# A spectral filter feeding a SwiGLU block: signs carried by the products instead of an in-place sign change, row scales sent at once, and an input fetch moved behind the second bounce

## The chip, the cores and the metric

The kernel runs on one core of a Trainium2 chip. The metric is the device time of one execution in microseconds (us), lower is better.

Engine names as the profile gives them: PE is TensorE (matmul), PEld its weight loads, DVE is VectorE, ACT is ScalarE, POOL is GpSimd, SP is SyncE, which here only issues DMAs.

## The reference

```python
X = np.fft.rfft(x, axis=1)                       # x: (8, 3008, 256) float32
Y = X * (filt_r + 1j * filt_i)[None]             # filters: (1505, 256)
x = np.fft.irfft(Y, n=3008, axis=1).reshape(8 * 3008, 256)
rms = np.sqrt(np.mean(x * x, axis=-1, keepdims=True) + 1e-06)
xn = x / rms * rms_g
g = xn @ w_gate                                  # (256, 1536)
out = (g / (1 + np.exp(-g)) * (xn @ w_val)) @ w_out
```

## The kernel before

The eight batches (called inputs too) go through one software pipeline. The feed-forward part of batch `b` fills TensorE, and the FFT of batch `b+1`, done as matmuls in two steps, is threaded between its pieces. One **slot** is one tile of 128 hidden features of a block of 512 tokens: four gate and value matmuls (`pg`, `pv`), and two slots later the `down` matmuls (`po`). A batch has 6 blocks of 12 slots, 72 slots. A plan says in which slot each piece of the FFT, the filter and the normalization is issued:

```python
items = [(b, m, jt) for b in range(B) for m in range(6) for jt in range(JT)]
...
for i in range(len(items) + 4):
    if i < len(items):
        gv(*items[i])                       # gate, value, silu, product
    for fn, a in plan.get(i, ()):           # the threaded pieces of slot i
        fn(*a)
    if 2 <= i < len(items) + 2:
        down(*items[i - 2])
    ...
    for fn, a in late.get(i, ()):           # q_unit only
        fn(*a)
```

The slots are only an order of issue: each engine works its own queue in that order and runs ahead until it must wait. In the profile of the kernel before, POOL had the block that slot 72 reads ready at 184.9 us, and PE came to it at 187.2. The pieces that matter here:

```python
def x_load(b, c):        # input fetch, issued by POOL: two DMAs a chunk, four chunks
def a_unit(b, i, ...):   # first transform: one matmul (psa), copied out by ACT or DVE to t1
def z_store(b, c):       # first bounce: t1 to DRAM, issued by SP; t1 has two buffers here
def t2_load(b, c):       # second bounce: back in the other layout, issued by SP

def b_unit(b, i):        # second transform and filter
    ps = bank(3, "psb")                     # one PSUM bank for all filter units
    ... two matmuls ...
    nc.vector.tensor_tensor(out=s1, in0=ps, in1=f1, op=ALU.mult)         # batches 2 to 7
    ...                  # batch 1: both products on DVE; for four units on POOL,
                         # from a copy v that ACT makes of the bank

def negate(c, r, n):     # called four times during batch 1
    t = fi[c][HALF:P, r:r + n, :]
    nc.gpsimd.tensor_scalar(out=t, in0=t, scalar1=-1.0, scalar2=None, op0=ALU.mult)

def swap_unit(b, i, h):  # batches 2 to 7: the crossed product, one half at a time
    a, e = ...           # 64 partitions out, the other 64 in
    nc.vector.tensor_tensor(out=s2[a], in0=ps[e], in1=f2[e], op=ALU.mult)
    if h:
        nc.gpsimd.tensor_tensor(out=s, in0=s1, in1=s2, op=ALU.add)

def bi_unit(b, i):       # inverse matmuls (psi), copied by ACT to t3 (two buffers)
def g_store(b, c):       # t3 to DRAM, issued by SP
def n_unit(b, m, dh):    # last inverse step of a block of 512 tokens

def q_unit(b, m):        # row sums of squares by PE, then
    nc.gpsimd.tensor_tensor(out=rho, in0=u, in1=mhalf, op=ALU.pow)
def rho_move(b, m):      # the row scale to DRAM, issued by POOL
def rho_load(b, m):      # back, spread over all partitions (rb), issued by SP
def xn_unit(b, m):       # POOL: xn = y * rb, the block that pg and pv read

def scale_split(m): ...  # the same spread without DRAM, by DVE and PE;
def scale_apply(m, bk):  # used for the first two blocks of batch 0 only
```

Batch 2's plan sets its filter units at `b_at = [71 + 3 * i ...]` and its first transform at `a_at = [51, 52, 53, 53, 54, 54, 55, 55, 56, 56, 57, 58]`; batch 3's fetch starts at slot 61.

## Time and profile before

| | before |
|---|---|
| median of the runs | 935.75 us (931.08 to 936.64, 4 runs) |
| span of the profiled run | 932.2 us |
| PE, DVE, ACT, POOL busy | 95%, 72%, 66%, 45% |

The page of the profile gives the span, and the busy time of each engine with its share of the span and its count of instructions:

```profile
span 932.2 us, 17516 instructions
...
PE 886.1 (95%) x6321; PEld 560.8 (60%) x6321; DVE 674.0 (72%) x1070; ACT 619.8 (66%) x1048; POOL 415.8 (45%) x359
```

PE is the bound: it is busy 299.3 of the 300 us from 500 to 800 us. What can be won lies before 215 us. The list of waits of PE alone, from 62 to 215 us, names it: who waited for what, us in total, how many times, the longest. In this kernel L263 is POOL's product of a filter unit, L241 a filter unit's matmul, L204 the first transform, L286 the inverse.

```profile
PE psi L286 <- POOL s L263: 6.9, 1, 6.9
PE psb L241 <- DMA t<-z_tmp: 5.5, 1, 5.5
PE psa L204 <- DVE t L207: 3.0, 1, 3.0
PE psi L286 <- POOL s L277: 2.0, 1, 2.0
```

These are the four stalls that the prediction calls S1, S3, S2 and S4, in this order. The timeline of POOL before S1 shows what kept it (start, duration, instruction; in brackets how long it stood idle before and what released it). L345 is the power that makes the row scale, L350 its sending, L405 the normalization, L269 the sign change:

```profile
90.21 1.03 POOL L345 TENSOR_TENSOR rho<-u,mhalf 128x4 f32<-128x4 f32 x1 [5.54 <-DVE u L343]
91.35 2.89 POOL L405 TENSOR_TENSOR xn<-y,rb 128x1024 f16<-128x1024 f32 x1
94.19 0.62 POOL L350 DMA_DIRECT2D r_tmp<-rho  x1
...
103.55 2.87 POOL L405 TENSOR_TENSOR xn<-y,rb 128x1024 f16<-128x1024 f32 x1 [4.67 <-DMA rb<-r_tmp]
...
108.15 5.39 POOL L269 TENSOR_SCALAR fi<-fi 64x2048 f32<-64x2048 f32 x1
113.62 1.26 POOL L263 TENSOR_TENSOR s<-v,fr 128x512 f16<-128x512 f32 x1
```

The scale of the power at 90.21 us is ready at 91.24 but is sent at 94.19 only, because the normalization of another block stands between. It is used at 103.55. Then comes the sign change, and only at 113.62 the product that PE needs. The table by windows shows the clock (the column after the bracketed counts is PEclk, then the DMA engines' busy share and GB/s; the first numbers are the window and the busy us of PE, PEld, DVE, ACT, POOL):

```profile
115.00:120.00 5.00, 4.16 (x16) 2.11 (x16) 1.29 (x2) 1.19 (x2) 4.78 (x6) 0.50 0.78 150
...
160.00:165.00 5.00, 2.27 (x8) 1.16 (x8) 1.98 (x3) 0.00 (x0) 0.00 (x0) 0.70 0.86 334
180.00:185.00 5.00, 0.68 (x5) 0.29 (x3) 1.05 (x2) 0.49 (x1) 2.99 (x2) 1.00 1.05 242
185.00:190.00 5.00, 3.83 (x15) 1.94 (x15) 1.45 (x3) 1.06 (x2) 1.74 (x4) 0.66 0.61 76
```

After S1, S2 and S3 the granted clock falls to 0.50 to 0.70, so in this profile each stall is paid for after it has ended, too. In the windows in which PE stands in S2 and S3 (160 and 180 us) the DMA engines are 0.86 and 1.05 busy.

### The profile page before, as it was taken

What the parts mean: (1) busy time and instruction counts of PE and PEld (TensorE: products, weight loads), DVE (VectorE), ACT (ScalarE), POOL (GpSimd) and SP (SyncE); (2) the same over time, 40 slices, a digit from 0 to 9 for tenths busy, and PEclk for the clock granted to TensorE, in tenths of its full rate; (3) what the DMA queues carried; (4) which work ended last, traced back from release to release, by engine and by line L of the source; (5) the groups of instructions that cost most, each with busy time, mean ns of one, the idle gap of its engine ahead of it and who ended that gap; (6) DMA issues with size and microseconds to landing.
All of it is one profiled execution on the core that took longest, in us unless ns stands there. A gap on an engine that the chain in (4) does not pass through costs nothing.

```text
span 932.2 us, 17516 instructions
## 1 busy us (share of the span) xinstructions
PE 886.1 (95%) x6321; PEld 560.8 (60%) x6321; DVE 674.0 (72%) x1070; ACT 619.8 (66%) x1048; POOL 415.8 (45%) x359
## 2 busy tenths in 40 slices
PE   8699698789999999999999999999999999999997
PEld 5565454556556666666666666666666666666554
DVE  7866465478888787787878887787878887555554
ACT  7667355557757776687657776687657775576543
POOL 7843774335633664256523555155522554033300
PEclk9999899999999999999999999999999999999999
DMA  9496736535555334553464345542353222321201
GB/s 200 83 169 165 127 65 166 136 71 147 118 143 158 79 96 144 156 110 106 91 179 109 97 97 116 155 101 84 72 173 83 63 63 71 100 63 46 69 24 45
DMA packets 79922, 101.17 MB, mean 109 GB/s; under 512 B 8144, under 2 KB 56464, under 8 KB 79452
## 3 DMA queue, kind: packets, MB, share of 16 engines
q1 hardware_dynamic: 69420, 83.71, 32.7%
q0 software_dynamic: 10416, 16.35, 11.4%
q8 instruction: 49, 0.80, 0.4%
q14 instruction: 37, 0.30, 0.1%
HBM read 67.93 MB, written 46.79 MB: 123 GB/s over the span
## 4 chain that ended last, share of the span: by engine, by line
PE 79%; DVE 6%; DMA 6%; POOL 4%; issue 3%; ACT 2%; SPq 0%; POOLq 0%; ACTq 0%; DVEq 0%
PE po L438 24%; PE pg L421 23%; PE pv L421 22%; DVE hh L426 3%; PE psb L241 2%; PE psi L286 2%; PE psn L318 2%; DMA fr<-in_filt_r_dram 2%; PE psa L204 2%; DMA rb<-r_tmp 2%; DVE o L444 1%; DVE s L274 1%; DMA t<-z_tmp 1%; PE psq L339 1%; POOL xn L405 1%
## 5 line engine op out<-in xcount | busy, mean ns | idle before, releaser
L426 DVE TENSOR_TENSOR hh<-pv,sg 128x512 f16<-128x512 f32 (+1 forms) x576 | 391.7, 680 | 216.3 <-ACT sg L425 103.3
L425 ACT ACTIVATE sg<-pg 128x512 f16<-128x512 f32 (+1 forms) x576 | 338.9, 588 | 248.8 <-PE pg L421 237.2
L438 PE MATMUL po<-wo,hh 128*128 128x256 f16 x2256 | 345.7, 273 | 2.7 <-DVE o L444 0.6
L421 PE MATMUL pg<-xn,wg 128*128 128x512 f16 (+1 forms) x1152 | 339.1, 376 | 0.6 <-POOL xn L405 0.4
L421 PE MATMUL pv<-xn,wv 128*128 128x512 f16 (+1 forms) x1152 | 338.7, 376 | 0.0
L438 PEld LDWEIGHTS <-hh 128*128 128x128 f16 x2256 | 217.4, 98 | 106.0 <-issue 10.4
L277 POOL TENSOR_TENSOR s<-s,s 128x512 f16<-128x512 f16 x96 | 110.5, 1151 | 291.8 <-DVE s L274 238.3
L421 PEld LDWEIGHTS <-wv 128*128 128x128 f16 x1152 | 112.8, 98 | 132.5 <-issue 2.5
L405 POOL TENSOR_TENSOR xn<-y,rb 128x1024 f16<-128x1024 f32 (+1 forms) x46 | 128.8, 2799 | 65.9 <-DMA rb<-r_tmp 59.0
L274 DVE TENSOR_TENSOR s<-psb,fi 64x512 f16<-64x512 f32 x192 | 132.1, 688 | 5.9
L421 PEld LDWEIGHTS <-wg 128*128 128x128 f16 x1152 | 109.4, 98 | 13.7 <-issue 1.3
L291 ACT ACTIVATE t<-psi 96x512 f16<-96x512 f32 x112 | 66.5, 593 | 21.1 <-PE psi L286 15.6
L345 POOL TENSOR_TENSOR rho<-u,mhalf 128x4 f32<-128x4 f32 (+1 forms) x48 | 48.7, 1014 | 69.6 <-DVE u L343 69.5
L324 ACT ACTIVATE y<-psn,gsb 128x512 f32<-128x512 f32 (+1 forms) x94 | 63.8, 679 | 9.0 <-PE psn L318 2.1
L247 DVE TENSOR_TENSOR s<-psb,fr 128x512 f16<-128x512 f32 x96 | 65.4, 681 | 5.9 <-PE psb L241 5.9
L330 ACT ACTIVATE sq<-psn 128x512 f16<-128x512 f32 (+1 forms) x94 | 54.7, 582 | 0.0
L286 PE MATMUL psi<-s,wi 128*128 128x256 f16 x248 | 45.9, 274 | 7.9 <-POOL s L263 6.9
L241 PE MATMUL psb<-t,wb 96*128 96x256 f16 x224 | 43.4, 275 | 9.3 <-DMA t<-z_tmp 5.5
L209 ACT ACTIVATE t<-psa 128x512 f16<-128x512 f32 x71 | 42.4, 597 | 9.5 <-PE psa L204 4.7
L286 PEld LDWEIGHTS <-wi 128*128 128x128 f16 x248 | 24.3, 98 | 36.0 <-issue 11.0
L318 PEld LDWEIGHTS <-t 128*128 128x128 f16 x368 | 28.4, 98 | 20.4 <-issue 0.4
L189 POOL DMA_DIRECT2D xc<-in_x_dram x64 | 34.4, 551 | 4.8 <-DMA wo<-in_moe_w_out_dram 1.3
(97 smaller groups left out, 494.0 us busy)
## 6 DMA issues: line engine op xcount, KB each, us to landing
out_dram<-o SPq DMA_DIRECT2D x84, 256.0 KB
xc<-in_x_dram POOLq DMA_DIRECT2D x56, 192.0 KB, 6.7
rb<-r_tmp SPq DMA_DIRECT2D x42, 256.0 KB
z_tmp<-t SPq DMA_DIRECT2D x28, 384.0 KB
t<-z_tmp SPq DMA_DIRECT2D x28, 384.0 KB
g_tmp<-t SPq DMA_DIRECT2D x56, 192.0 KB
t<-g_tmp SPq DMA_DIRECT2D x21, 384.0 KB
out_dram<-o SPq DMA_DIRECT2D x12, 192.0 KB
```

What stands on the lines that cost most here:

```text
L241: nc.tensor.matmul(ps[:, u, :], w[:, k, :], t, start=True, stop=True)
L247: nc.vector.tensor_tensor(out=s1, in0=ps, in1=f1, op=ALU.mult)
L274: nc.vector.tensor_tensor(out=s2[a], in0=ps[e], in1=f2[e], op=ALU.mult)
L277: nc.gpsimd.tensor_tensor(out=s, in0=s1, in1=s2, op=ALU.add)
L286: nc.tensor.matmul(ps[:, u, :], wi_at(q, 2 * i + u), ss[q][:, u, :], start=(q == 0), stop=(q == n - 1))
L291: nc.scalar.activation(out=st[b]["t3"][c][:, 2 * r:2 * r + 2, :], in_=ps[0:KR], func=AXT.Copy)
L324: nc.scalar.activation(out=y[:, dh, 0:w], in_=ps[:, 0:w], func=AXT.Identity, scale=gsb[:, dh:dh + 1])
L405: nc.gpsimd.tensor_tensor(out=xv, in0=yv, in1=rv.unsqueeze(1).to_broadcast([P, 2, n, P]), op=ALU.mult)
L421: nc.tensor.matmul(ps[:, 0:w], wt[:, dt_, ts(jt, P)], xn[:, dt_, 0:w], start=(dt_ == 0), stop=(dt_ == 1))
L425: nc.scalar.activation(out=sg[:, 0:w], in_=pg[:, 0:w], func=AXT.Silu)
L426: nc.vector.tensor_tensor(out=hh[:, 0:w], in0=pv[:, 0:w], in1=sg[:, 0:w], op=ALU.mult)
L438: nc.tensor.matmul(po[s4 // 2][:, s4 % 2, :], hh[:, ts(s4, P)], wo[:, jt, :], start=(jt == 0 and s4 % 2 == 0), stop=(jt == JT - 1 and (s4 ...
```

## The change

Three parts. The sign moves into the product: one of the two crossed products becomes a `scalar_tensor_tensor` with -1, and the four sign changes on POOL go. The row scale is sent by POOL right behind its power, and in batches 0 and 1 loads and uses come one slot later. Batch 3's fetch moves from slot 61 to 73, behind the second bounce of batch 2; with it batch 2's first transform is stretched, its second bounce comes two slots and its first filter unit one slot later, and one block of batch 1 is normalized earlier.

```diff
-    def negate(c, r, n):
-        t = fi[c][HALF:P, r:r + n, :]
-        nc.gpsimd.tensor_scalar(out=t, in0=t, scalar1=-1.0, scalar2=None, op0=ALU.mult)
 ...
     def swap_unit(b, i, h):
-        nc.vector.tensor_tensor(out=s2[a], in0=ps[e], in1=f2[e], op=ALU.mult)
+        if h:
+            nc.vector.tensor_tensor(out=s2[a], in0=ps[e], in1=f2[e], op=ALU.mult)
+        else:
+            nc.vector.scalar_tensor_tensor(out=s2[a], in0=ps[e], scalar=-1.0, in1=f2[e],
+                                           op0=ALU.mult, op1=ALU.mult)
 ...                                     # end of q_unit; rho_move goes
-        st[b]["u"][m] = rho
+        if b or m > 1:
+            nc.gpsimd.dma_start(r_d[b, m, 0:n * P]..., rho[:, 0:n])
+        else:
+            st[b]["u"][m] = rho
 ...                                     # slots of power, sending, load, use
-            norm_plan(0, m, s0, s0 + 2, r)                     # r = (2, 3, 4, 7)
+            norm_plan(0, m, s0, s0 + 2, (2, 5, 8))
-                          (2, 4, 6, 10) if b > 1 else (2, 3, 4, 7))
+                          (2, 6, 10) if b > 1 else (2, 5, 8))
 ...                                     # batch 1
-                n_at, n_step = [58, 62, 74, 86, 95, 107], 3
+                n_at, n_step = [58, 62, 66, 86, 95, 107], 3    # and step 2 for m < 3
 ...                                     # batch 2
-                a_at = [51, 52, 53, 53, 54, 54, 55, 55, 56, 56, 57, 58]
-                on_dve = (0, 1, 3, 5, 7, 9, 10, 11)
-                b_at = [71 + 3 * i for i in range(16)]
+                a_at = [51, 52, 53, 53, 54, 54, 57, 57, 58, 59, 60, 61]
+                on_dve = (0, 1, 3, 5, 7, 8, 9, 10, 11)
+                b_at = [72] + [71 + 3 * i for i in range(1, 16)]
 ...                                     # batch 3: first transform, fetch
-                a_at = [72, 73, 80, 81, 83, 84, 92, 93, 101, 102, 104, 105]
+                a_at = [77, 78, 80, 81, 83, 84, 92, 93, 101, 102, 104, 105]
-                at(b_at[0] - (5 if b == 1 else 7) + ... t2_load, b, c)
+                at(b_at[0] - (5, 6, 7)[min(b, 3) - 1] + ... t2_load, b, c)
-                at(s0 + lag, bi_unit, b, i)
-                if b == 1 and i in (3, 7, 11, 15):
-                    at(s0 + 2, negate, i // 4, 0, 8)
+                at(s0 + lag - (b == 2 and i == 0), bi_unit, b, i)
-                    at((24, 61)[b - 1] + 2 * c if b < 3 else ..., x_load, b + 1, c)
+                    at((24, 73)[b - 1] + 2 * c if b < 3 else ..., x_load, b + 1, c)
```

More of the change, by code (lines that the diff above doesn't have):

```diff
@@ L345, in q_unit @@
         nc.gpsimd.tensor_tensor(out=rho[:, 0:n], in0=u[:, 0:n], in1=mhalf[:, 0:n], op=ALU.pow)
-        st[b]["u"][m] = rho
-    def rho_move(b, m):
-        n = nq(b, m)
-        nc.gpsimd.dma_start(r_d[b, m, 0:n * P].rearrange("(p q) -> p q", q=n),
-                          st[b]["u"].pop(m)[:, 0:n])
+        if b or m > 1:
+            nc.gpsimd.dma_start(r_d[b, m, 0:n * P].rearrange("(p q) -> p q", q=n), rho[:, 0:n])
+        else:
+            st[b]["u"][m] = rho
     def rho_load(b, m):
@@ L698, in norm_plan @@
                 at((s0, s1)[dh] + 1, sq_unit, b, m, dh)
-            for d, fn in zip(r, (q_unit, rho_move, rho_load, xn_unit)):
+            for d, fn in zip(r, (q_unit, rho_load, xn_unit)):
                 at(s1 + d, fn, b, m)
@@ L708 @@
         at(20, open_sp)
-        for m, s0, r in ((2, 4, (2, 3, 4, 7)), (3, 15, (2, 3, 4, 7)), (4, 19, (2, 3, 4, 7)),
-                         (5, 23, (2, 3, 4, 7))):
-            norm_plan(0, m, s0, s0 + 2, r)
+        for m, s0 in ((2, 4), (3, 15), (4, 19), (5, 23)):
+            norm_plan(0, m, s0, s0 + 2, (2, 5, 8))
         for b in range(1, B):
@@ L737 @@
             for c in range(4):
-                at(b_at[0] - (5 if b == 1 else 7) + (1 if b == 1 else 2) * c if c < 3 else b_at[4] + 1,
+                at(b_at[0] - (5, 6, 7)[min(b, 3) - 1] + (1 + (b > 1)) * c if c < 3 else b_at[4] + 1,
                    t2_load, b, c)
@@ L752 @@
                 for c in range(NXC):
-                    at((24, 61)[b - 1] + 2 * c if b < 3 else a_at[3 * c + 2] + 2, x_load, b + 1, c)
+                    at((24, 73)[b - 1] + 2 * c if b < 3 else a_at[3 * c + 2] + 2, x_load, b + 1, c)
             for c in range(4):
@@ L756 @@
             for m in range(6):
-                step = 2 if b == 1 and m < 2 else n_step
+                step = 2 if b == 1 and m < 3 else n_step
                 norm_plan(b, m, n_at[m], n_at[m] + step,
-                          (2, 4, 6, 10) if b > 1 else (2, 3, 4, 7))
+                          (2, 6, 10) if b > 1 else (2, 5, 8))
         stores = {}
```

## The prediction

> **What bounds the kernel now.** TensorE. The profile page gives PE 886.1 us busy in a span of 932.2 (95%), DVE 72%, ACT 66%, POOL 45%. The table by windows gives PE at least 99.7% busy in each 100 us from 400 to 800 us: nothing to win there. Of the idle PE, about 14 us lie in the first 62 us, untouched, and about 22 us between 62 and 200 us. Its waits and timeline name four stalls there:
>
> - S1, 107.7 to 116.2 us: PE waits 6.92 and 0.84 us for POOL's products of the second input. POOL was late: it waited for a row scale (xn at 103.55; its scale was sent at 94.19 only, behind the xn at 91.35, though the power ended at 91.2), then did one in-place sign change of 5.39 us.
> - S2, 157 to 162.7 us: 0.93 + 3.04 us for evictions that wait for the first bounce (z store) of batch 2, 6.85 us in flight while the 16 DMA engines are full (share 1.0, 267 to 334 GB/s), partly with batch 3's input.
> - S3, 180.7 to 186.2 us: 5.49 us for the second bounce's load, 10.26 us in flight, behind four input fetches issued at 174.2 (DMA share 1.05).
> - S4, 196 to 197.4 us: 2.04 us for POOL's add behind an xn that waited 6.63 us for its row scale.
>
> After S1 to S3 the granted clock is about half for 3 to 6 us (windows: 0.50, 0.70, 0.66). [...] I estimate that S1 costs 10.9, S2 5.2, S3 7.5 and S4 2.1 us: 25.7 in all.
>
> **What changes.** Removed: four sign changes (5.4 us each, 21.5 us of POOL); only the first is on the critical path. Added: nothing on PE; 96 tensor_tensor of 64x512 (688 ns) on DVE become scalar_tensor_tensor. [...] I expect 0.69 us still. Moved: each row scale's DMA follows its power directly (about 3 us sooner for batch 0's fifth); batch 2's last two chunks of the first transform 3 to 4 slots later; the second bounce's loads 2 slots, its use 1 slot later; batch 3's fetch 12 slots later, behind those loads, its use 5 slots later.
>
> **Gains.** S1: POOL's product should be ready near 106.5, before PE asks at 107.7: about 10.5 won. S2: about 4.5. S3: about 6.5. S4: about 2. New costs: batch 3's first fetch is now only 4 slots (about 7.5 us) ahead of its use, behind an xn on POOL, with 6.3 us from issue to landing in this region: a PE wait of 2 to 3 us there, and small waits for POOL's first adds. Net about 20.5 us.
>
> **Predicted: 915 us, 8 in 10 between 908 and 925.** Faster by over 2%: 0.57; within 2%: 0.42; slower: 0.01.
>
> **Shown right by**: no 6.9 us PE wait on POOL; no PE wait over 2 us on the second bounce; clock above 0.95 from 105 to 200 us; DVE swaps all at 0.69 us; PE busy 99.7% later. **Wrong if**: the fetch of batch 3 stalls PE over 4 us (throttling it again); [...] the z stores are slow anyway.

## More of the kernel before

A verdict of "faster" needs 2%.

## The result, and the profile after

| | before | after |
|---|---|---|
| median of the runs | 935.75 us (931.08 to 936.64, 4 runs) | 919.98 us (919.79 to 921.92, 4 runs) |
| ratio | | 0.9851, 95% interval 0.9819 to 0.9883 |
| span of the profiled run | 932.2 us | 918.0 us |

Ratios here and below are taken from the runs of the same rounds. They are not quite the ratio of the quoted medians, which is 0.983 here. The interval lies clear of 1: about 1.5% less.

The page after. Line numbers after the sign change's place are 2 lower than before (L421 is L419, L405 is L403), and the swapped products are L273 and L271 where they were L274.

```profile
span 918.0 us, 17505 instructions
...
PE 885.4 (96%) x6321; PEld 561.2 (61%) x6321; DVE 674.5 (73%) x1071; ACT 619.7 (68%) x1047; POOL 394.8 (43%) x355
```

PE's busy time has not changed (886.1 and 885.4 us). The 14 us came out of its idle time. The list of PE's waits from 62 to 215 us:

```profile
PE psb L241 <- DVE s L271: 3.1, 4, 2.4
PE pg L419 <- POOL xn L403: 2.4, 1, 2.4
...
PE psa L204 <- DMA xc<-in_x_dram: 0.8, 1, 0.8
```

None of the four lines shown of before is left. In their place stand a wait for POOL's normalization, and waits of a filter unit for DVE. POOL's timeline at the place of S1:

```profile
93.27 1.03 POOL L345 TENSOR_TENSOR rho<-u,mhalf 128x4 f32<-128x4 f32 x1 [5.53 <-DVE u L343]
94.60 0.60 POOL L347 DMA_DIRECT2D r_tmp<-rho  x1 [0.29 <-POOL rho L345]
...
96.25 2.92 POOL L403 TENSOR_TENSOR xn<-y,rb 128x1024 f16<-128x1024 f32 x1
...
103.89 2.92 POOL L403 TENSOR_TENSOR xn<-y,rb 128x1024 f16<-128x1024 f32 x1
106.71 1.32 POOL L263 TENSOR_TENSOR s<-v,fr 128x512 f16<-128x512 f32 x1
```

The scale is sent at 94.60, 0.3 us after its power has ended, ahead of the normalization. The next normalization (103.89) finds its scale landed, no sign change follows, and the product is started at 106.71. The windows answer to those of before, the first at S1, the other at the new waits:

```profile
110.00:115.00 5.00, 5.00 (x36) 3.32 (x35) 3.55 (x6) 2.90 (x6) 2.71 (x3) 1.00 1.02 216
...
170.00:175.00 5.00, 3.46 (x13) 1.70 (x13) 1.29 (x2) 0.66 (x2) 3.10 (x3) 0.66 0.23 64
```

The clock is full at S1, but 0.66 from 170 to 175 us. The timeline of PE shows what stands there (from 175 to 180 us, where the clock is 1.00, a pair of gate matmuls of this size takes 0.59 us):

```profile
171.54 1.01 PE L419 MATMUL pg<-xn,wg 128*128 128x512 f16 x2 [2.44 <-POOL xn L403]
...
178.94 0.39 PE L241 MATMUL psb<-t,wb 96*128 96x256 f16 x2 [2.41 <-DVE s L271]
...
184.95 0.38 PE L204 MATMUL psa<-xc,tb 128*128 128x512 f16 x1 [0.78 <-DMA xc<-in_x_dram]
```

Three new waits stand there: 2.44 us for the first normalized block of batch 1 (L419, slot 72), 2.41 us of batch 2's second filter unit for DVE (L241, slot 74), and 0.78 us for batch 3's fetch (L204). The first of them, and why it was late, on POOL:

```profile
159.56 1.03 POOL L345 TENSOR_TENSOR rho<-u,mhalf 128x4 f32<-128x4 f32 x1 [23.59 <-DVE u L343]
160.89 0.64 POOL L347 DMA_DIRECT2D r_tmp<-rho  x1 [0.30 <-POOL rho L345]
...
168.64 2.85 POOL L403 TENSOR_TENSOR xn<-y,rb 128x1024 f16<-128x1024 f32 x1 [2.58 <-DMA rb<-r_tmp]
```

The power at 159.56 is followed at once by its sending (160.89), and the scale lands in DRAM at 162.7. SP issues its load at 162.77 and two loads of the second bounce at 163.3 and 163.7. From 165 to 170 us the DMA engines are 1.01 busy, and the normalization (168.64), which waits for the scale's load, ends at 171.5.

To see where the time went, one can take from each trace the start of the first gate matmul of some slots. The table gives the length of a stretch in the two profiled runs of each kernel (the second pair are the runs `before_again` and `after_again` of below), and the difference of the means:

| stretch | before, two runs | after, two runs | difference |
|---|---|---|---|
| start to slot 34 | 107.0, 110.4 | 110.0, 109.6 | +1.1 |
| 34 to 40 (S1) | 21.4, 19.7 | 10.8, 10.8 | -9.8 |
| 40 to 60 (S2) | 39.4, 38.2 | 33.4, 33.4 | -5.4 |
| 60 to 71 | 12.1, 12.1 | 13.8, 13.8 | +1.7 |
| 71 to 72 (S3) | 7.3, 7.2 | 3.6, 3.3 | -3.8 |
| 72 to 75 | 5.9, 6.3 | 8.1, 8.4 | +2.1 |
| 75 to 77 (S4) | 5.0, 4.8 | 2.8, 2.8 | -2.1 |
| 77 to 84 (fetch of batch 3) | 11.9, 11.9 | 13.4, 14.1 | +1.8 |
| 84 to 575 | 714.1, 714.2 | 714.1, 714.2 | 0.0 |

The sum is -14.4 us. S1, S2 and S4 gave what the prediction said, within 1 us. From slot 60 to 84, where it expected 6 us (6.5 for S3, 2 for S4, less 2.5 for the fetch), 0.3 us were won. Some of that is only moved work: the plan puts pieces of the transform and of the normalization into slots 60 to 71 that stood elsewhere. In `after_a_early` below, which moves the pieces of the transform back, the stretch from 60 to 71 is 12.8 us, 1.0 less.

### The profile page after: what moved, and what is told of

Same layout as the page of the kernel before. It is cut to its first block, busy times and chain, and to the rows that moved or that the text cites. A ratio compares the mean times of both kernels' runs of the same rounds, so it can differ in the third digit from the quotient of the medians.

```text
span 918.0 us, 17505 instructions
## 1 busy us (share of the span) xinstructions
PE 885.4 (96%) x6321; PEld 561.2 (61%) x6321; DVE 674.5 (73%) x1071; ACT 619.7 (68%) x1047; POOL 394.8 (43%) x355
## 4 chain that ended last, share of the span: by engine, by line
PE 79%; DVE 6%; issue 6%; DMA 5%; POOL 2%; ACT 2%; SPq 0%; POOLq 0%; DVEq 0%; ACTq 0%
PE po L436 23%; PE pg L419 23%; PE pv L419 22%; DVE hh L424 2%; PE psb L241 2%; PE psi L286 2%; DMA fr<-in_filt_r_dram 2%; PE psn L318 2%; PE psa L204 2%; DVE o L442 2%; PE psq L339 1%; DVE s L271 1%; DMA r_tmp<-rho 1%; ACT sg L423 1%; POOL xn L403 1%
## 5 line engine op out<-in xcount | busy, mean ns | idle before, releaser
L419 PE MATMUL pg<-xn,wg 128*128 128x512 f16 (+1 forms) x1152 | 338.6, 375 | 3.0 <-POOL xn L403 2.8
L419 PE MATMUL pv<-xn,wv 128*128 128x512 f16 (+1 forms) x1152 | 338.6, 376 | 0.0
L419 PEld LDWEIGHTS <-wv 128*128 128x128 f16 x1152 | 112.8, 98 | 132.1 <-issue 1.8
L403 POOL TENSOR_TENSOR xn<-y,rb 128x1024 f16<-128x1024 f32 (+1 forms) x46 | 128.8, 2801 | 50.0 <-DMA rb<-r_tmp 36.3
L419 PEld LDWEIGHTS <-wg 128*128 128x128 f16 x1152 | 109.2, 98 | 16.1 <-issue 3.9
L273 DVE SCALAR_TENSOR_TENSOR s<-psb,fi 64x512 f16<-64x512 f32 x96 | 66.6, 693 | 3.0
L271 DVE TENSOR_TENSOR s<-psb,fi 64x512 f16<-64x512 f32 x96 | 65.6, 684 | 3.0
L241 PE MATMUL psb<-t,wb 96*128 96x256 f16 x224 | 43.2, 274 | 6.7 <-DVE s L271 5.1
```

Of the source, the lines that this page charges most:

```text
L273: nc.vector.scalar_tensor_tensor(out=s2[a], in0=ps[e], scalar=-1.0, in1=f2[e], op0=ALU.mult, op1=ALU.mult)
L403: nc.gpsimd.tensor_tensor(out=xv, in0=yv, in1=rv.unsqueeze(1).to_broadcast([P, 2, n, P]), op=ALU.mult)
L419: nc.tensor.matmul(ps[:, 0:w], wt[:, dt_, ts(jt, P)], xn[:, dt_, 0:w], start=(dt_ == 0), stop=(dt_ == 1))
```

## The experiments

Each ran beside the kernel before on the same chip.

### The same two kernels again: `before_again`, `after_again`

No edit.

> The kernel before once more, unchanged, for its trace. In the profile of the changed kernel the first feed-forward slot starts 1.7 us and the 20th slot 3.1 us later than in the profile of before, and in the three runs of single parts 1.5 to 2.0 us later, though nothing in these stretches was changed. Theory: that is the spread of the start from run to run (filter loads, clock grants), so this run too differs from the first profile of before by 1 us or more at the 20th slot. Rival: the change slows the start, and this run agrees with the first profile within 0.5 us. Ratio 0.998 to 1.002.

> The changed kernel once more, as the control for the runs beside it: ratio 0.983 to 0.988; 2.4 us wait for the first normalized block of batch 1 and 2.4 us for the second filter unit of batch 2 as in its first profile; start at the 20th slot within 1.5 us of it or not, as for the kernel before.

Measured: 933.94 us, ratio 0.9994 (0.9971 to 1.0018), and 921.23 us, ratio 0.9863 (0.9838 to 0.9889). Slot 20 of the kernel before started at 82.3 us in its first profile and at 85.7 in this one; the changed kernel's two were 85.4 and 84.9. So the start varies by some 3 us from run to run, and the change is not shown to slow it. There is something more to read: `before_again` was 3.4 us later at slot 34 and only 0.6 us later at the end. S1 and S2 took 2.9 us less in it: PE's waits ended 2.2 us later than in the first profile at S1 (117.16 against 114.93) and 1.8 at S2 (164.55 against 162.73), and the first pair of gate matmuls after S2 took 0.59 us in place of 1.06. So here the two stalls took up most of the late start. The table above therefore uses two runs of each.

### One part of the change alone: `signs_only`, `scales_only`, `fetch_only`

Edits: the kernel before with the first part of the diff (the product carries the sign, no sign changes), with the second (scales sent at once, their slots), or with the third (everything in the plan of batches 1, 2 and 3). The three together are the whole change, word for word.

> The kernel before with the first part of the change alone: no sign changes in place, the swapped products carry the sign. Theory: the first stall (TensorE waits 6.92 + 0.84 us for GpSimd's products of the second input) is mostly the 5.39 us sign change ahead of them[...]. Then the wait shrinks to 1 to 3 us, the clock stays full, and the span falls by 7 to 9 us; the other three stalls stay. Rival: GpSimd was late already for its row scale, so removing the sign change leaves 4 us or more of wait and the throttle, and saves under 5 us. The new DVE form takes 0.69 us and costs nothing.

> The kernel before with the second part alone: the row scale is sent by GpSimd right after its power, loads and uses one slot later. The sign changes stay. Theory: the row scale of the fifth block of batch 0 leaves 3 us sooner, so the normalization before the sign change ends about 2.5 us sooner; the first stall shrinks from 6.9 to 3 to 5 us; the fourth stall (2.04 us for GpSimd's add behind a late normalization) is gone; span 4 to 7 us less. Rival: DMA congestion, not the late sending, decides when the scale arrives, and the span falls by less than 2 us.

> The kernel before with the third part alone: batch 3's fetch 12 slots later, the last two chunks of batch 2's first transform later, second bounce 2 slots and its use 1 slot later, the third block of batch 1 normalized earlier. Sign changes and late scales stay. Theory: the stall for the first bounce (3.96 us and the half clock) and the 5.49 us wait for the second bounce's load both go, but the latter is replaced, as in the changed kernel, by a wait for the first normalized block of batch 1 (2 to 4 us, since its row scale lands about 8 us after its power) and one of about 2.4 us for the second filter unit, which now comes 2 slots after the first; net 6 to 9 us less. Rival: without the earlier row scales the normalization waits get longer than 5 us and this part alone saves less than 4 us. The first stall stays at 6.9 us.

| | median | ratio to before (95%) |
|---|---|---|
| signs_only | 934.93 us | 0.9985 (0.9935 to 1.0035) |
| scales_only | 931.83 us | 0.9942 (0.9894 to 0.999) |
| fetch_only | 934.80 us | 0.9976 (0.9932 to 1.002) |
| the whole change, two measurements | 919.98 and 921.23 us | 0.9851, 0.9863 |

The ratios of the parts fall by 0.15%, 0.58% and 0.24%, together 1.0%, and the whole change's by 1.4 to 1.5%. The first and the third are not told apart from nothing, and both fell short of their expectations; the second's 0.58% is 5.4 us, within the expected 4 to 7. But the intervals are wide, since two of the runs of the kernel before in these rounds took 940 and 941 us: by the ratios alone the parts might still add up to the whole. The medians say otherwise: against the 934.41 us of the same rounds the parts gave +0.5, -2.6 and +0.4 us, the whole in its own rounds -15.8 and -12.6. The profiles, one of each part, show why: each part takes one wait away and another comes forward in the same few slots.

*signs_only* did take the 6.9 us wait away. PE waited 0.9 us for the second of the two products instead. But some 10 us later it stood for 5.4 us. The line of PE's timeline, and the line of ACT's waits that explains it:

```profile
121.88 0.58 PE L241 MATMUL psb<-t,wb 96*128 96x256 f16 x2 [5.42 <-ACT v L261]
```

```profile
ACT t L291 <- DMA g_tmp<-t: 6.1, 1, 6.1
```

ACT could not empty PSUM into `t3`, since the store of `t3`'s other contents had not landed, and so it came late to the copy `v` that frees the bank PE wanted. That store stands on SP behind the load of a row scale. SP's timeline in this run, then in the changed kernel:

```profile
110.74 0.33 SPq L356 DMA_DIRECT2D rb<-r_tmp  x1
...
111.64 1.46 SPq L294 DMA_DIRECT2D g_tmp<-t  x2
```

```profile
107.96 0.33 SPq L354 DMA_DIRECT2D rb<-r_tmp  x1
...
108.86 3.60 SPq L294 DMA_DIRECT2D g_tmp<-t  x2
```

The scale's load (L356, L354 after) waits until the scale that POOL sends (at 106.92 us here, 102.23 in the changed kernel) has landed, 3.8 and 5.7 us later. It goes out at 110.74 us here and at 107.96 in the changed kernel, whose start was 1.3 us later; the stores behind it follow, 0.9 us later in both timelines. I read from these two that the load, while it waits, holds back the stores queued after it: ACT had filled the stored half of `t3` at 105.8 here, and its store left at 111.64. That is not all of the delay. ACT could go on at 120.7 us here and at 114.9 in the changed kernel, 9.1 and 6.0 us after the store was issued, so 3 us of the 5.9 are a longer flight, whose cause is open. In the kernel before the same late store (111.78) was hidden behind S1. So the time of S1 had two causes side by side, the sign change on POOL and the late store behind the late scale on SP, and in these runs it went only when both did. My theory for this run named one of them.

*scales_only* and *fetch_only* in the lists of PE's waits from 62 to 330 us:

```profile
PE pg L419 <- POOL xn L403: 6.4, 2, 6.0
...
PE psi L286 <- POOL s L263: 2.6, 1, 2.6
```

```profile
PE psi L286 <- POOL s L263: 5.7, 1, 5.7
...
PE psi L286 <- POOL s L277: 3.8, 2, 2.9
```

In *scales_only* S1 shrank to 2.6 us for the first product and S4 is gone, as expected. But with the fetch still early, PE waits 6.0 us for the normalized block of batch 1. In *fetch_only* S1 stays, the wait for the bounce is gone, and PE then waits 3.8 us for POOL's adds of batch 2: POOL sends a scale at 177.5 us, behind a normalization, and waits 6.2 us for it before it can come to the adds.

### The fetch early, or the first transform early, in the changed kernel: `after_fetch61`, `after_a_early`

```diff
-  at((24, 73)[b - 1] + 2 * c ..., x_load, b + 1, c)               # after_fetch61
+  at((24, 61)[b - 1] + 2 * c ..., x_load, b + 1, c)
```
```diff
-  a_at = [51, 52, 53, 53, 54, 54, 57, 57, 58, 59, 60, 61]         # after_a_early
+  a_at = [51, 52, 53, 53, 54, 54, 55, 55, 56, 56, 57, 58]         # on_dve without 8
```

> The changed kernel with batch 3's input fetched as early as in the kernel before (slot 61 on), all else as changed. Theory: the fetches run beside the second bounce's load and the row scales again, so the first normalized block or the filter units of batch 2 wait 2 to 5 us longer: ratio 0.988 to 0.992. Rival: moving the loads and uses by one or two slots was what mattered, the order of fetch and bounce does not, and the ratio stays at 0.984 to 0.987 or falls, since the wait of about 1 us for the fetch itself goes.

> The changed kernel with the last two chunks of batch 2's first transform in the slots of the kernel before (55 to 58), the fetch still late. Theory: the second stall comes from asking for the transposed buffers before the first bounce has emptied them; it returns with 2 to 4 us of TensorE waits, in part with the half clock, ratio 0.987 to 0.992. Rival: the stall came from the fetch in the same window; with the fetch gone the stores land sooner, the waits stay under 1.5 us, and the earlier stores even help the second bounce: ratio 0.982 to 0.986.

Measured: `after_fetch61` 925.21 us, ratio 0.9892 (0.987 to 0.9913); `after_a_early` 921.70 us, ratio 0.9861 (0.9839 to 0.9883). Their PE waits, in this order:

```profile
PE pg L419 <- POOL xn L403: 5.9, 2, 5.6
...
PE psb L241 <- ACT v L261: 2.2, 1, 2.2
```

```profile
PE psb L241 <- ACT v L261: 1.9, 1, 1.9
PE psa L204 <- DVE t L207: 1.3, 1, 1.3
```

With the fetch early the wait for the normalized block is 5.6 us instead of 2.4, and slots 71 to 75 take 15.9 us instead of 11.7. So for S3 the theory holds: there the third part wins by keeping batch 3's fetch off the DMA engines while the second bounce and the row scales use them. (The profiled run of `after_fetch61`, at 928.30 us, was the slowest of its four.) The early first transform costs nothing that the ratio shows: of S2's 3.04 us, 1.29 come back, and 1.9 of the 5.4 us of slots 40 to 60. There the rival holds: with the fetch late, stretching the first transform was not needed.

But S2 was not the fetch alone. `after_fetch61` has a fetch in the first bounce again, 0.4 us ahead of a store (147.75 and 148.11; in the kernel before 152.20 and 152.56). POOL's timeline there:

```profile
147.75 1.11 POOL L189 DMA_DIRECT2D xc<-in_x_dram  x2 [8.70 <-PE psa L204]
```

From 150 to 160 us the DMA engines are 0.94 to 0.97 busy, and yet no wait of S2 is in its list, and slots 40 to 60 take only 0.9 us more than in the changed kernel. So the stretched transform without the late fetch cures S2 as well: either of the two is enough for most of it.

Both lists also hold a wait for ACT's copy `v` (2.2 and 1.9 us), the one of `signs_only` in small, in slots where both kernels are the same as the changed one. It varies from run to run, so the store behind the scale's load is only just in time.

### The two new waits: `after_spaced`, `after_onchip`, `after_bank`, `onchip_bank`

All four are the changed kernel with an edit. The filter units of batch 2 lie at slots 72, 74, 77: moving only the first made a gap of two slots.

```diff
-  b_at = [72] + [71 + 3 * i for i in range(1, 16)]                # after_spaced
+  b_at = [72, 75, 78] + [71 + 3 * i for i in range(3, 16)]
```
```diff
-            ps = bank(3, "psb")                                   # after_bank
+            ps = bank(0 if (b, i) == (2, 0) else 3, "psb")
```
```diff
 # after_onchip: batch 1's first block uses scale_split and scale_apply (given a batch
 # argument) at slots 65 and 67, in place of sending, load and POOL's normalization
-        if b or m > 1:
+        if (b, m) != (1, 0) and (b or m > 1):
 ...
+                if (b, m) == (1, 0):
+                    at(65, scale_split, 0, 1)
+                    at(67, scale_apply, 0, 3, 1)
```

`onchip_bank` has the edits of `after_onchip` and `after_bank`.

> The changed kernel with the second and third filter unit of batch 2 one slot later each, so that units one and two are 3 slots apart again instead of 2. Theory: the 2.41 us wait of the second unit follows from the 2 slots: one PSUM bank serves both, and VectorE's last product of the first unit stands in the slot in which TensorE asks. Then that wait falls under 0.5 us and the span by 1.5 to 2.4 us against the changed kernel. Rival: the wait is an aftermath of the late start of that block (half clock, VectorE behind), and at least 1.5 us of it stay.

> The changed kernel with the row scale of batch 1's first block spread over the partitions by TensorE and VectorE, as batch 0's first two blocks do already, instead of the trip through DRAM and GpSimd. Theory: the 2.44 us wait for GpSimd's normalized block and the half clock after it come from the scale's trip (power at 159.6, landed at 168.6, normalized at 171.5 us in the changed kernel's profile); without the trip the wait is gone; TensorE pays 8 small matmuls, about 0.5 us; span 2 to 4 us less than the changed kernel. Rival: the second bounce's load lands no sooner than the normalized block, so TensorE waits for it instead and under 1 us is saved.

> The changed kernel with the first filter unit of batch 2 in another PSUM bank than the second; no slot is moved. Theory: the 2.41 us wait of the second unit is for the one bank that VectorE has not yet emptied, two slots after the first; with its own bank it is gone and the span falls by 1.5 to 2.4 us against the changed kernel's runs. Rival (the spaced run made nothing faster): the wait stands for VectorE's queue as a whole and comes back at the third unit or at GpSimd's adds, and under 0.7 us is saved.

> The changed kernel with both remedies: the row scale of batch 1's first block spread on the chip, and the first filter unit of batch 2 in another bank. Theory: the two waits are independent of each other, so the savings add: 5 to 7 us less than the changed kernel, ratio to the kernel before 0.977 to 0.980; no TensorE wait above 1 us is left between 62 and 240 us. Rival: GpSimd's adds or the fetch for batch 3 become the next wait and under 4.5 us is saved.

| | median | ratio to before (95%) |
|---|---|---|
| after_spaced | 922.19 us | 0.9878 (0.9854 to 0.9903) |
| after_onchip | 916.68 us | 0.9804 (0.9779 to 0.9828) |
| after_bank | 920.62 us | 0.9859 (0.983 to 0.9887) |
| onchip_bank | 916.27 us | 0.9808 (0.9784 to 0.9832) |

*after_spaced*: the second unit's wait fell from 2.41 to 0.20 us, but my edit left a gap of two slots between the third and the fourth, and the wait was there. PE's timeline:

```profile
179.85 0.38 PE L241 MATMUL psb<-t,wb 96*128 96x256 f16 x2 [0.20 <-DVE s L271]
...
191.98 0.38 PE L241 MATMUL psb<-t,wb 96*128 96x256 f16 x2 [1.62 <-DVE s L271]
```

The place of the wait follows the short gap, and the time did not fall.

*after_onchip*: PE no longer waits for the normalized block at slot 72, and 4.6 us are gone against the median of `after_again` in the same rounds. By the traces it is 3.5 us from slot 40 to 84, and two waits of `after_again` account for it: 2.13 us for the block, and 1.48 us for the fetch, which POOL now issues sooner, having one normalization less to do. The half clock did not go, it moved: slots 72 to 75 took 1.7 us less, slots 75 to 77 1.7 us more, for now pairs of 1.06 us follow the wait of the second unit. That wait stayed as it was, so it is no aftermath of the late block:

```profile
174.91 0.39 PE L241 MATMUL psb<-t,wb 96*128 96x256 f16 x2 [2.41 <-DVE s L271]
```

*after_bank* took that wait away and nothing clear of noise was won, as the rival said: POOL's adds and the fetch, issued by POOL too, took its place.

```profile
182.47 0.27 PE L286 MATMUL psi<-s,tb 128*128 128x256 f16 x1 [2.91 <-POOL s L277]
...
186.27 0.38 PE L204 MATMUL psa<-xc,tb 128*128 128x512 f16 x1 [1.91 <-DMA xc<-in_x_dram]
```

*onchip_bank*: the waits for block and bank are gone, and the saving is that of `after_onchip` alone. In the profiled run, the slowest of the four, the next wait is for the fetch (L204):

```profile
182.84 0.38 PE L204 MATMUL psa<-xc,tb 128*128 128x512 f16 x1 [2.36 <-DMA xc<-in_x_dram]
```

So in this stretch, to judge by these waits of 1.9 to 2.9 us, three chains end within about 3 us of each other: the row scale's way through DRAM, DVE's queue with one PSUM bank, and POOL with adds, a normalization and the fetch. Taking one or two away shows the next.

### A version with all three: `onchip_bank_fetch71`

```diff
-  at((24, 73)[b - 1] + 2 * c ..., x_load, b + 1, c)               # onchip_bank with
+  at((24, 71)[b - 1] + 2 * c ..., x_load, b + 1, c)
```

> Both remedies and batch 3's fetch two slots earlier (slot 71), so that GpSimd issues it ahead of the second normalized block of batch 1 instead of behind it. Theory: with the first two waits gone the next one is the fetch itself (2.36 us in the run with both remedies); its first chunk then leaves about 3 us sooner, that wait is gone, and the ratio to the kernel before is 0.976 to 0.979. Rival: the fetch again meets the second bounce and the row scales on the DMA engines, the waits move there, and the ratio stays at 0.980 or above.

Measured over five rounds: 913.95 us (912.51 to 915.73), ratio to the kernel before 0.978 (0.9762 to 0.9799): the lowest of all. The interval still overlaps that of `onchip_bank`; what the trace shows is that the fetch's wait of 2.36 us is gone. The fetch is issued at 169.4 us, ahead of the normalization at 170.4. Of PE's waits from 62 to 330 us no single one of over 1.5 us is left. The first line of the list:

```profile
PE psb L241 <- DVE s L271: 2.3, 5, 1.5
```

Its longest wait, 1.5 us near slot 120, stands in the kernel before too.

## Why the prediction was right or wrong

**Right.** PE was the bound, and the waits of 62 to 215 us were where time could come from: after slot 84 both kernels take the same time to 0.1 us. S1 gave 9.8 us (10.5 predicted), S2 5.4 (4.5), S4 2.1 (2). The new DVE form costs what the old one did; the groups of DVE after the change (count, busy us, mean ns):

```profile
L273 DVE SCALAR_TENSOR_TENSOR s<-psb,fi 64x512 f16<-64x512 f32 x96 | 66.6, 693 | 3.0
L271 DVE TENSOR_TENSOR s<-psb,fi 64x512 f16<-64x512 f32 x96 | 65.6, 684 | 3.0
```

The measured median, 919.98 us, lies in the range of 908 to 925; that owes something to the range's width, since one term failed. The verdict held to be likeliest, faster by over 2% (0.57), did not come. The fetch's own wait was 0.8 and 1.5 us in the two profiles, where I said 2 to 3.

**Wrong in size.** The forecast gain of 20.5 us was too large: 15.8 us came by the medians, 14.4 by the traces. The step that failed is the term "S3: about 6.5". The wait for the second bounce did go, as the prediction said. But from slot 71 to 75 only 1.7 us were won, because S3 hid one wait and the change made another:

- The first normalized block of batch 1 is due at slot 72 as well. In the kernel before it was ready at 184.9 us and PE, held by S3, came to it at 187.2. With S3 gone PE came first, and waited 2.44 us, and ran at half clock (pairs of 1.01 and 1.06 us, where 0.59 is the full clock's). The prediction looked at what PE waited for, and not at what else was due at the end of the wait. `after_onchip` shows that removing this wait saves time.
- The change moves the first filter unit "1 slot later", as the prediction has it, and not the second. The prediction did not see that this leaves the bank two slots: with two the waits were 2.41 us here and 1.62 in `after_spaced`, with three 0.20 in `after_spaced`. `after_spaced` and `after_bank` show the wait to be one for the bank; `after_bank` shows as well that its removal alone is worth nothing clear of noise.

Two statements were too simple though the sum came out: "only the first [sign change] is on the critical path" (so is, beside it, the late scale on SP; `signs_only` saved nothing clear of noise), and S2's cure, which I put down to the later slots and the fetch together, where either was enough for most of it (`after_fetch61`, `after_a_early`). Of the things that would show it right, "no 6.9 us PE wait on POOL" and "no PE wait over 2 us on the second bounce" came true, as did the 0.69 us of the DVE forms and PE's later share (299.3 of the 300 us from 500 to 800), "clock above 0.95 from 105 to 200 us" did not (0.66 from 170 to 175).

**Shown and argued.** That the parts need each other is shown by the medians of the three single runs and by the waits in their profiles; their ratios alone leave it open. That the late store of `signs_only` comes from the scale's load ahead of it on SP is read from two timelines; no run moved the store alone, and 3 us of its delay stay unexplained. Of the +1.7 us of slots 60 to 71, 1.0 goes when the transform's pieces move back (`after_a_early`); where the rest came from was not measured apart.

## What to carry to other kernels

Before adding up the waits of a bound engine, ask of each what else is due when it ends: the second-latest input sets what its removal is worth. When several queues feed one stretch of the plan, the parts of a change can each measure as little or nothing and together as 14 us, so try them together before dropping one. And when a piece moves by a slot, look at the gap to the next one that shares its buffer.

## What the traces show of the clock, the new product and the row scales

- Waits of 2.44 and 2.13 us (the changed kernel's two profiles) were followed by gate matmul pairs of 1.01 us, where 0.59 is the full clock's, and one of 2.47 us (`after_bank`) was not. A wait of 2.41 us was followed by pairs of 1.06 us in `after_onchip` and of 0.59 in the changed kernel; the one of S2 by pairs of 1.06 us after 3.04 us in the kernel before, and of 0.59 after 3.06 us in `before_again`. In these runs the length of a wait of 2.1 to 3.1 us did not tell whether it cost the clock.
- `scalar_tensor_tensor` with one fp32 source in PSUM and one in SBUF took 693 ns for 64x512, against 684 ns for `tensor_tensor` (the changed kernel).
- The 46 row scales of 1.5 to 2 KB that POOL sends landed 1.8 us after their issue in the median of the kernel before. But one sent at 106.36 us, just ahead of two input fetches, took 4.5 us, and one of the changed kernel, sent at 165.46 (the DMA engines were 1.01 busy from 165 to 170 us), took 7.0.
